# Filler products ahead of waiting TensorE steps: 78 more in the first fifth of an RWKV-7 and SwiGLU kernel

## The chip, the cores and the metric

One core of one Trainium2 chip. The metric is the device time of one execution in microseconds (us), as the median of several runs.

## The reference

Two blocks in a row, all in float32.

```python
# r, k, v, w, a, b: (4 batches, 8 heads, 768 steps, 40)
for t in range(S):
    y[:, :, t] = einsum('bhd,bhde->bhe', rt, state)
    Sa = einsum('bhde,bhe->bhd', state, at)
    state = state * wt[:, :, None, :] - einsum('bhd,bhe->bhde', Sa, bt)
    state = state + einsum('bhd,bhe->bhde', vt, kt)
x = y as (3072 tokens, 320)
xn = x / sqrt(mean(x * x) + 1e-6) * rms_g
out = (silu(xn @ w_gate) * (xn @ w_val)) @ w_out      # 320 -> 1536 -> 320
```

The three weight matrices of the FFN come as float64 and are made float32 on the chip.

## The kernel before, in words

The recurrence is cut into 24 chunks of 32 steps. For a chunk `c` the program makes four groups of steps:

- `front(c)`: loads of `w`, `a` into `wan`, of `k`, `b` into `kbn`, of `v` into `VU` (four loads for `wan`, four for `kbn`, eight for `VU`; from chunk 2 on they stand in POOL's queue), transposes of them by TensorE (`turn`), and for each of the five levels 1, 2, 4, 8, 16 a Gram product (`gram`, 32 matmul records in the trace) whose operand `KE` is copied by ScalarE and whose result is masked into `LT` by VectorE and copied into `KN` by ScalarE. The products by the decays (`K`, `A`, `T`) are VectorE's.
- `early_inverse(c)` for chunks 0 to 3, `inverse(c)` for the others: a triangular inverse, row by row on VectorE (`tmp`, then `Yi` or `M`), after `LT` has gone to DRAM (`sB`) and come back (`M`) through SP's queue; in the early form two TensorE steps (`inv`) put two half inverses together.
- `main(c)`: products with the state (`state`), with `LT` (`lower`), the update of the state (`update`), the scores of `r` (`score`), the output level by level (`y0`, `level`; VectorE adds them up in `y`), and then the transposes `turn4` and `turn3` around the normalisation (ScalarE squares, POOL takes the power, `ss`), which end in the FFN's input `xg`.
- After every second chunk `feed(g)`: the FFN for 256 tokens over twelve slices of the weights: `h64` and `h` (gate and value), `sg` by ScalarE, `hT` by VectorE, and `out`, which accumulates in the PSUM tile `po`.

In the first two chunks there are also 24 `narrow` steps: the weights are loaded as pairs of 32-bit words and made float32 by ScalarE (`ex`) and VectorE (`w`).

The steps are not issued in this order. The functions only note them down as pieces of a plan; `Plan.issue` then goes through the list `ORDER`, written out ahead of time, and issues one piece after the other. Each number counts from the first piece that has not been issued. Each engine works through its own pieces in the order of issue, so that list is the order of every engine and of every queue (SP, ACT and POOL issue the loads). Semaphores are put in by the framework where a piece reads or overwrites what another has made.

A piece that needs PSUM has a "room" of one or two banks; `PAIRS` has one digit for each of the 523 rooms, and says in which of the three bank pairs (0, 2, 4) it lies. The first piece of a room waits until the last reader of the room before it in that bank pair is done.

The sign `-` in `ORDER` is a filler: it calls `plan.warm`, a product of the identity with itself into columns 320 to 447 of `po`, which nothing reads.

```python
            if word == "-":
                self.order.append(None)
                self.warm()
                continue
```

```python
plan.warm = lambda: nc.tensor.matmul(po_[:, 0, DM:DM + P], ident, ident, start=False, stop=False, skip_group_check=True)
```

A float32 product appears in the trace as two records, so a filler is two LDWEIGHTS and two MATMUL of 128x128 by 128x128. The kernel before has 28 fillers: seven ahead of the first FFN step, the rest spread up to the end.

Helpers are recorded under one line each, so the trace's lines read: L499 products, L502 transposes, L1014 fillers (all TensorE); L457 VectorE; L477, L480, L483 ScalarE (activation, copy, scale); L486, L489, L492 POOL; L496 loads and stores.

Of the kernel before, what the change touches and what calls it, by code (L numbers as in the profile page):

```python
# [36 lines left out]
199 96 112 105 61 66 111 115 119 106 116 130 120 117 118 129 - 200 107 121 212 222 211 232 242 131 204 205 208 209 210  # L37
193 472 477 221 35 134 476 132 62 206 213 489 219 207 490 470 471 321 0 216 217 122 43 125 64 124 222 213 - 191 219 214
# [4 lines left out]
501 510 506 503 493 508 517 514 507 519 515 21 22 321 - 520 516 322 263 518 193 817 502 511 521 - 512 525 529 398 1003  # L43
# [5 lines left out]
32 37 406 405 408 293 349 317 - 832 318 1 956 834 418 419 839 344 404 833 598 845 843 409 841 410 350 421 558 559 424  # L49
# [6 lines left out]
428 429 432 589 590 419 408 594 593 592 986 859 591 595 543 596 597 422 598 599 409 600 922 980 - 982 925 854 855 862  # L56
# [9 lines left out]
277 385 222 80 278 769 122 303 279 0 385 279 120 12 122 11 373 575 82 83 222 223 224 232 13 14 307 359 280 386 71 - 281  # L66
387 16 388 389 231 17 0 554 765 430 375 376 60 65 555 556 0 209 764 763 563 264 558 265 562 374 0 374 375 564 376 558
287 100 207 210 211 284 559 377 563 572 265 560 565 571 427 65 1 2 3 0 - 62 570 565 262 1001 425 263 569 562 578 374
375 579 0 0 0 560 202 692 199 207 60 561 208 61 563 577 0 0 371 0 371 372 373 374 375 227 228 376 377 571 565 378 570
59 206 207 420 422 421 569 575 423 379 61 62 380 381 382 383 384 579 385 424 - - 425 - 427 276 271 1 0 0 0 0 381 382 58  # L70
579 0 560 - 0 573 0 380 420 560 577 573 418 381 575 - 568 680 - 578 382 383 559 581 569 582 384 580 595 250 570 385 584
574 386 579 528 527 - 423 431 594 425 424 589 588 387 388 389 390 391 392 393 434 394 395 427 1 2 3 0 0 428 424 421 2
677 680 0 0 44 - 0 387 419 421 423 47 587 426 0 426 427 431 673 674 587 241 714 718 736 242 576 577 428 719 982 715 254
# [3 lines left out]
694 - 943 944 945 360 392 393 394 565 745 395 0 608 691 611 609 610 612 357 709 694 562 697 563 698 692 695 925 461 693  # L77
# [969 lines left out]
```

## Time and profile before

| | |
|---|---|
| median of 3 runs | 933.53 us (932.12 to 934.17) |
| profiled execution | 934.43 us, span from first to last instruction 932.6 us |
| TensorE (PE) busy | 875.3 us, 94% of the span, 22072 matmuls |
| weight loads (PEld) | 700.9 us, 75% |
| VectorE (DVE) busy | 728.2 us, 78% |
| ScalarE (ACT) busy | 522.2 us, 56% |
| GpSimd (POOL) busy | 297.6 us, 32% |
| mean granted TensorE clock | 0.970 |

Read the shares by stages: until about 116 us the recurrence's first chunks and the weights' narrowing share all engines, later the FFN fills TensorE. The busy time of a matmul is from its start to its modelled end, and matmuls overlap; so a burst is read by its start, its length and its count. The clock column says which share of TensorE's full clock was granted, where the trace has a record of it.

### The profile page before, as it was taken

The numbers are of one execution on the slowest core, as the hardware profiler recorded it, in microseconds if no ns is written. First come the engines' busy times: TensorE is split into PE (matmuls) and PEld (weight loads), VectorE is DVE, ScalarE is ACT, GpSimd is POOL, SyncE is SP. The second block draws the span as 40 slices with busy tenths as digits, with TensorE's granted clock in tenths as the row PEclk, the third lists the DMA queues.
The fourth block names the chain that finished last, engine by engine and source line by source line (L and its number), as shares of the span: only waits on it lengthen the run. The fifth ranks groups of instructions, "written<-read, shape, count | busy, mean of one in ns | idle before, by whom it ended". The sixth has DMA issues, their size and how long they took to land.

```text
span 932.6 us, 50209 instructions
## 1 busy us (share of the span) xinstructions
PE 875.3 (94%) x22072; PEld 700.9 (75%) x22072; DVE 728.2 (78%) x2702; ACT 522.2 (56%) x1144; POOL 297.6 (32%) x515
## 2 busy tenths in 40 slices
PE   4766799899999999999999999999999999999998
PEld 4665677678777778778887877778777778777786
DVE  6887889778878988889888887888888878774411
ACT  6887877764574564666556456547455454432211
POOL 7676555413232333233324212514403230020000
PEclk9995599989999999999999999999999999999999
DMA  8654556342233233234323303414404222021000
GB/s 155 111 104 106 126 117 123 79 81 64 48 76 66 52 69 67 53 70 91 68 47 70 77 18 77 94 24 84 93 13 92 59 44 58 7 59 29 2 15 15
DMA packets 146362, 63.00 MB, mean 68 GB/s; under 512 B 128800, under 2 KB 138080, under 8 KB 146144
## 3 DMA queue, kind: packets, MB, share of 16 engines
q1 hardware_dynamic: 125664, 29.46, 16.7%
q0 software_dynamic: 18368, 30.01, 14.7%
q8 instruction: 173, 2.83, 1.3%
q10 hardware_dynamic: 2112, 0.33, 0.3%
q14 instruction: 45, 0.37, 0.1%
HBM read 49.15 MB, written 10.09 MB: 64 GB/s over the span
## 4 chain that ended last, share of the span: by engine, by line
PE 63%; DVE 11%; ACT 9%; issue 7%; DMA 5%; POOL 3%; SPq 1%; DVEq 0%; ACTq 0%; POOLq 0%
PE ps L499 44%; PE po L499 12%; PE ps L502 6%; DVE tmp L457 2%; DMA w<-in_moe_w_out_dram 2%; DVE Yi L457 2%; ACT VU L480 1%; DVE y L457 1%; DVE hT L457 1%; ACT KE L480 1%; SPq L496 1%; DVE w L457 1%; DVE K L457 1%; ACT ex L477 1%; POOL w L496 1%
## 5 line engine op out<-in xcount | busy, mean ns | idle before, releaser
L499 PE MATMUL ps<-xg,w 128*128 128x256 f32 (+1 forms) x1728 | 355.1, 394 | 2.4 <-DVE tmp L457 1.0
L499 PEld LDWEIGHTS ps<-xg,w 128*128 128x128 f32 (+1 forms) x1728 | 265.3, 192 | 51.6 <-issue 12.0
L499 PE MATMUL po<-w,hT 128*128 128x320 f32 x576 | 178.4, 445 | 0.0
L496 POOL DMA_DIRECT2D VU<-in_v_dram x184 | 102.4, 561 | 136.9 <-PE ps L499 97.7
L457 DVE TENSOR_TENSOR tmp<-Yi,M 128x60 f32<-128x60 f32 (+24 forms) x620 | 129.3, 209 | 15.5 <-DMA M<-sB 2.7
L457 DVE TENSOR_TENSOR Yi<-Yi,tmp 128x60 f32<-128x60 f32 (+24 forms) x620 | 129.8, 210 | 14.1 <-DMA rn<-in_r_dram 0.3
L480 ACT COPY KE<-K 128x512 f32<-128x512 f32 x168 | 110.6, 661 | 44.2 <-DVE K L457 36.7
L477 ACT ACTIVATE sg<-ps 128x256 f32<-128x256 f32 x144 | 52.8, 385 | 142.2 <-PE ps L499 133.1
L499 PEld LDWEIGHTS po<-w,hT 128*128 128x128 f32 x576 | 103.6, 189 | 36.7 <-issue 1.3
L457 DVE TENSOR_TENSOR hT<-ps,sg 128x256 f32<-128x256 f32 x144 | 58.6, 420 | 74.5 <-ACT sg L477 72.7
L457 DVE TENSOR_TENSOR K<-K,T 128x256 f32<-128x256 f32 x240 | 98.3, 420 | 13.2 <-ACT KE L480 10.7
L499 PE MATMUL ps<-A,KE 40*64 40x72 f32 x3840 | 94.5, 246 | 13.5 <-ACT A L480 3.9
L499 PEld LDWEIGHTS ps<-A,KE 40*64 40x64 f32 x3840 | 78.5, 148 | 34.1 <-ACT A L480 8.5
L480 ACT COPY KN<-ps 128x320 f32<-128x320 f32 x144 | 67.1, 470 | 63.6 <-DVE LT L457 26.7
L457 DVE COPY_PREDICATED LT<-msk,ps 128x256 f32<-128x256 uint32 x120 | 65.9, 549 | 21.0 <-PE ps L499 16.1
L486 POOL TENSOR_TENSOR ss<-ss,mhalf 128x1 f32<-128x1 f32 x24 | 17.9, 745 | 187.5 <-DVE ss L457 186.3
L457 DVE TENSOR_TENSOR y<-y,ps 128x256 f32<-128x256 f32 x119 | 49.8, 419 | 15.5 <-PE ps L499 12.9
L457 DVE TENSOR_TENSOR A<-A,T 128x128 f32<-128x128 f32 (+1 forms) x168 | 56.0, 337 | 2.7 <-ACT A L480 1.7
L496 POOL DMA_DIRECT2D kbn<-in_k_dram x44 | 29.1, 663 | 85.8 <-PE ps L502 79.7
L499 PEld LDWEIGHTS ps<-As,KN 64*40 64x40 f32 x3840 | 45.8, 123 | 14.1 <-issue 5.1
L499 PE MATMUL ps<-As,KN 64*40 64x32 f32 x3840 | 51.9, 205 | 3.9 <-ACT y L480 1.8
L480 ACT COPY VU<-ps 32x320 f32<-32x320 f32 x96 | 40.0, 417 | 13.9 <-PE ps L499 12.7
(121 smaller groups left out, 1245.0 us busy)
## 6 DMA issues: line engine op xcount, KB each, us to landing
M<-sB SPq DMA_DIRECT2D x80, 128.0 KB, 3.3
rn<-in_r_dram SPq DMA_DIRECT2D x24, 160.0 KB, 3.6
out_dram<-o SPq DMA_DIRECT2D x48, 80.0 KB, 2.9
VU<-in_v_dram POOLq DMA_DIRECT2D x184, 20.0 KB, 2.7
kbn<-in_b_dram POOLq DMA_DIRECT2D x44, 80.0 KB, 3.6
kbn<-in_k_dram POOLq DMA_DIRECT2D x44, 80.0 KB, 3.6
wan<-in_w_dram POOLq DMA_DIRECT2D x44, 80.0 KB, 3.1
wan<-in_a_dram POOLq DMA_DIRECT2D x44, 80.0 KB, 3.1
```

Source lines behind the costliest of these rows:

```text
L457: plan.add("DVE", kind, lambda at: fn(at(o), *m(at)), [o], aps(*args))
L477: plan.add("ACT", "act", lambda at: nc.scalar.activation(at(o), at(a), f, **kw), [o] + aps(acc), [a])
L480: plan.add("ACT", "copy", lambda at: nc.scalar.copy(at(o), at(a)), [o], [a])
L486: plan.add("POOL", "tt", lambda at: nc.gpsimd.tensor_tensor(o, a, b, op), [o], [a, b])
L496: plan.add(by, "dma", lambda at: queue.dma_start(out=o, in_=i), [o], [i])
L499: return o, lhsT, rhs, lambda at: nc.tensor.matmul(at(o), lhsT, rhs, start=start, stop=stop, skip_group_check=True)
L502: return o, i, ident, lambda at: nc.tensor.transpose(at(o), i, ident)
```

## The change

`ORDER` gets 78 more `-`, at 25 places; with the `-` taken out, the list of numbers is the same in both. `PAIRS` differs in 94 of its 523 digits. All code is the same. The places, by the TensorE step that the new fillers stand in front of, in order of issue:

| in front of | new fillers |
|---|---|
| `front(0)` transpose of `KE`; `front(1)` Gram level 1, level 4, level 8; `front(3)` first transpose | 7; 3, 3, 4; 3 |
| `main(0)` first `lower`; `front(2)` Gram level 1, level 4; `early_inverse(0)` first, second `inv`; `front(2)` Gram level 16 | 7; 1, 2; 3, 2; 1 |
| `main(0)` transpose of `VU`, `score`, first `level` | 5, 4, 2 |
| `front(3)` second transpose, Gram level 1 | 1, 6 |
| `main(1)` transpose of `VU`, `score`, first `level`, `turn4`, `turn3` | 2, 1, 3, 8, 3 |
| `main(3)` second `lower`, `update` | 3, 2 |
| `front(5)` Gram level 8; `main(3)` `level` for level 1 | 1; 1 |

The diff, cut to its core (the numbers are the same throughout; the lines are broken anew):

```diff
-199 96 112 105 61 66 111 115 119 106 116 130 120 117 118 129 - 200 107 121 212 222 211 232 242 131 204 205 208 209 210
-193 472 477 221 35 134 476 132 62 206 213 489 219 207 490 470 471 321 0 216 217 122 43 125 64 124 222 213 - 191 219 214
...
+199 96 112 105 61 66 111 115 119 106 116 130 120 117 118 129 - 200 107 121 212 222 211 232 242 - - - - - - - 131 204 -
+- - 205 208 209 210 193 472 477 221 35 134 476 132 62 206 213 489 219 207 490 470 471 321 0 216 217 122 43 125 64 124
+222 213 - 191 219 214 123 - - - 223 229 226 227 230 215 232 490 228 238 236 237 66 242 224 126 127 134 239 135 240 - -
+- - 233 247 243 234 373 374 136 137 138 139 140 141 142 818 474 822 381 225 819 823 35 473 244 - - - 835 143 246 144
...
```

```diff
 PAIRS = """
-20404244230204042223024024202204224244423024242422242000000400040454220222424244000044242440444042200044020420420224240
+20404244230204042223024024202204224244423024242422242000000400040454220222424244000044242440444042200044020240420224240
...
```

Taken room by room in the order of issue, 12 rooms get another predecessor in their bank pair, in six pairs of rooms that swap: two in `front(5)`, one in `main(3)` and one in `main(4)`, then `main(18)` with `feed(7)`, `front(21)` with `main(19)` twice, and `main(21)` with `main(22)`.

More of the change, by code (lines that the diff above doesn't have):

```diff
@@ L36 @@
 92 103 94 90 85 201 370 34 98 77 19 99 100 87 262 133 473 86 102 202 113 104 186 187 101 108 109 203 95 97 110 114 198
-199 96 112 105 61 66 111 115 119 106 116 130 120 117 118 129 - 200 107 121 212 222 211 232 242 131 204 205 208 209 210
-193 472 477 221 35 134 476 132 62 206 213 489 219 207 490 470 471 321 0 216 217 122 43 125 64 124 222 213 - 191 219 214
[4 rows of a table removed]
-501 510 506 503 493 508 517 514 507 519 515 21 22 321 - 520 516 322 263 518 193 817 502 511 521 - 512 525 529 398 1003
[5 rows of a table removed]
-32 37 406 405 408 293 349 317 - 832 318 1 956 834 418 419 839 344 404 833 598 845 843 409 841 410 350 421 558 559 424
+199 96 112 105 61 66 111 115 119 106 116 130 120 117 118 129 - 200 107 121 212 222 211 232 242 - - - - - - - 131 204 -
+- - 205 208 209 210 193 472 477 221 35 134 476 132 62 206 213 489 219 207 490 470 471 321 0 216 217 122 43 125 64 124
+222 213 - 191 219 214 123 - - - 223 229 226 227 230 215 232 490 228 238 236 237 66 242 224 126 127 134 239 135 240 - -
+- - 233 247 243 234 373 374 136 137 138 139 140 141 142 818 474 822 381 225 819 823 35 473 244 - - - 835 143 246 144
+145 146 147 148 149 150 235 258 319 62 1006 195 245 257 151 152 153 251 154 155 156 157 158 397 1002 485 259 836 837
+248 260 63 491 486 30 388 254 67 253 - - - - - - - 310 159 160 161 162 163 252 164 165 166 487 311 376 499 196 190 262
+496 495 249 167 500 498 509 504 505 121 - 492 497 255 256 494 501 510 506 503 493 508 517 514 507 519 515 21 22 321 -
+520 516 322 263 518 193 817 502 - - 511 521 - 512 525 529 398 1003 168 513 522 524 170 174 173 172 176 530 382 19 46
+389 25 - - - 177 377 535 527 178 375 169 523 526 383 189 534 378 528 264 265 266 267 268 269 270 271 31 272 820 29 23
+273 171 175 - - 179 180 391 274 275 538 194 24 50 - 531 545 399 392 312 314 315 316 313 - - - - - 325 546 326 - - - -
+329 532 384 323 324 49 821 385 402 386 533 330 331 - - 336 276 277 278 279 537 280 281 282 283 1007 339 415 400 541 284
+285 407 20 1343 338 286 287 288 289 394 290 416 547 548 401 393 291 335 332 292 47 337 540 539 542 544 333 334 403 340
+395 536 838 396 341 343 543 549 550 551 552 553 554 345 555 556 557 342 346 347 417 420 348 250 48 816 32 37 406 405
+408 293 349 317 - - 832 318 1 956 834 418 419 - - - - - - 839 344 404 833 598 845 843 409 841 410 350 421 558 559 424
 483 957 294 295 560 840 351 296 844 411 425 426 51 423 484 427 428 422 842 846 847 352 297 599 303 300 2 601 433 478
@@ L52 @@
 270 376 819 825 393 827 271 1231 813 377 828 829 526 822 272 824 320 985 837 527 378 528 529 838 530 531 826 831 396
[3 rows of a table removed]
-428 429 432 589 590 419 408 594 593 592 986 859 591 595 543 596 597 422 598 599 409 600 922 980 - 982 925 854 855 862
[9 rows of a table removed]
-277 385 222 80 278 769 122 303 279 0 385 279 120 12 122 11 373 575 82 83 222 223 224 232 13 14 307 359 280 386 71 - 281
-387 16 388 389 231 17 0 554 765 430 375 376 60 65 555 556 0 209 764 763 563 264 558 265 562 374 0 374 375 564 376 558
-287 100 207 210 211 284 559 377 563 572 265 560 565 571 427 65 1 2 3 0 - 62 570 565 262 1001 425 263 569 562 578 374
@@ L69 @@
[L69 to L73, printed above, removed]
[3 rows of a table removed]
@@ L77 @@
-694 - 943 944 945 360 392 393 394 565 745 395 0 608 691 611 609 610 612 357 709 694 562 697 563 698 692 695 925 461 693
[27 rows of a table removed]
-1002 455 1008 1006 946 860 861 859 810 862 811 1015 1016 1162 812 450 - 451 1156 863 813 864 814 815 865 866 867 868
[14 rows of a table removed]
-844 841 436 - 437 843 845 799 442 800 438 982 1095 848 992 983 801 995 993 682 846 851 1003 1001 1002 802 852 984 669
-1008 1012 838 996 430 1139 945 944 685 1142 853 1138 803 1154 - 1000 1009 839 1155 994 1156 854 855 856 1010 1140 1135
[3 rows of a table removed]
-1024 450 1168 445 1171 - 438 1085 942 1025 1175 1181 446 1026 1027 938 1182 1095 669 1180 1028 1194 818 817 816 819
[36 rows of a table removed]
@@ L162 @@
-1051 1192 1217 1178 1052 1093 - 449 1179 669 1187 1053 1054 1188 1055 1189 1395 1056 943 1057 999 1104 1108 1058 1109
-1191 450 451 1059 1060 1106 670 1105 1107 1196 439 443 1203 1061 1193 671 1112 1111 1062 869 870 1110 1144 944 1399
-1197 1114 1063 1064 1198 1113 448 1199 1065 1115 1116 1117 1412 1066 1067 1068 1205 1069 453 1409 1604 1121 1201 941
-942 938 1070 1071 1200 939 1601 1208 1207 1413 1414 1206 1118 1120 1119 - 458 454 1072 1073 1074 1122 1411 1213 1214
-1123 1124 1125 1126 1410 0 452 1420 1073 456 1287 457 453 1072 1207 1206 1208 1209 1212 1199 1412 1213 1285 - 868 1416
[6 rows of a table removed]
@@ L173 @@
-1154 1155 1156 799 800 1398 999 1006 1005 850 851 801 852 802 425 803 804 805 856 857 858 859 - 430 860 861 806 837
[9 rows of a table removed]
-1599 942 941 1067 1202 1209 1208 1211 458 1410 1409 1214 1414 1068 1069 1070 1071 1072 1201 453 447 - 451 454 1215 1073
[53 rows of a table removed]
-280 268 273 277 281 282 285 286 297 292 288 293 289 301 298 302 294 290 291 295 303 299 300 304 0 233 - 0 129 226 227 1
-0 0 225 222 0 0
+273 417 532 823 566 832 567 570 568 569 399 984 400 836 833 - - 573 533 835 426 424 425 443 841 839 534 535 536 537 538
+539 842 843 402 847 834 540 574 401 844 852 853 420 541 542 403 968 964 860 840 846 845 404 321 324 418 423 861 965 -
@@ new lines @@
+577 579 583 580 585 588 581 323 322 407 406 856 427 587 857 421 578 405 850 851 969 - - - 586 444 441 1228 611 858 584
+582 430 431 428 429 432 589 590 419 408 594 593 592 986 859 591 595 543 596 597 422 598 599 409 600 922 980 - 982 925
+854 855 862 924 412 544 413 - - - - - - - - 601 923 981 410 994 602 411 987 571 637 612 603 564 638 640 414 572 546 629
+630 604 991 639 848 605 606 - - - 607 608 609 909 910 613 992 545 610 863 990 993 864 616 865 1004 866 867 868 869 614
[8 rows of a table added]
+13 14 307 359 280 386 71 - 281 387 16 388 389 231 17 0 554 765 430 375 376 60 65 555 556 0 209 764 763 563 264 558 265
@@ new lines @@
+562 374 0 374 375 564 376 558 287 100 207 210 211 284 559 377 563 572 265 560 565 571 427 65 1 2 3 0 - 62 570 565 262
+1001 425 263 569 562 578 374 375 579 0 0 0 560 202 692 199 207 60 561 208 61 563 577 0 0 371 0 371 372 373 374 375 227
+228 376 377 571 565 378 570 59 206 207 - - - 420 422 421 569 575 423 379 61 62 380 381 382 383 384 579 385 424 - - - -
+425 - 427 276 271 1 0 0 0 0 381 382 58 579 0 560 - 0 573 0 380 420 560 577 573 418 381 575 - - 568 680 - 578 382 383
+559 581 569 582 384 580 595 250 570 385 584 574 386 579 528 527 - 423 431 594 425 424 589 588 387 388 389 390 391 392
@@ new lines @@
+393 434 394 395 427 1 2 3 0 0 428 424 421 2 677 680 0 0 44 - 0 387 419 421 423 47 587 426 0 426 427 431 673 674 587 241
+714 718 736 242 576 577 428 719 982 715 254 978 730 432 387 388 257 389 243 429 433 434 244 573 732 - 430 737 435 731
+436 1139 437 438 740 439 582 583 515 1 0 533 534 0 0 471 391 932 3 689 540 541 694 542 543 392 693 695 526 690 342 610
+611 343 544 545 546 547 548 549 550 551 552 341 344 692 553 705 554 702 4 5 555 0 392 346 0 611 554 555 556 557 558 559
+560 561 562 563 564 346 343 263 924 925 344 694 - 943 944 945 360 392 393 394 565 745 395 0 608 691 611 609 610 612 357
[27 rows of a table added]
@@ new lines @@
+809 689 858 1161 1013 1160 454 1002 455 1008 1006 946 860 861 859 810 862 811 1015 1016 1162 812 450 - 451 1156 863 813
[14 rows of a table added]
+792 793 794 795 796 850 797 798 842 844 841 436 - 437 843 845 799 442 800 438 982 1095 848 992 983 801 995 993 682 846
+851 1003 1001 1002 802 852 984 669 1008 1012 838 996 430 1139 945 944 685 1142 853 1138 803 1154 - 1000 1009 839 1155
[3 rows of a table added]
+1019 1020 1167 1083 1021 1022 1023 740 1024 450 1168 445 1171 - 438 1085 942 1025 1175 1181 446 1026 1027 938 1182 1095
[36 rows of a table added]
+1177 1186 1184 1190 1194 1195 1051 1192 1217 1178 1052 1093 - 449 1179 669 1187 1053 1054 1188 1055 1189 1395 1056 943
@@ new lines @@
+1057 999 1104 1108 1058 1109 1191 450 451 1059 1060 1106 670 1105 1107 1196 439 443 1203 1061 1193 671 1112 1111 1062
+869 870 1110 1144 944 1399 1197 1114 1063 1064 1198 1113 448 1199 1065 1115 1116 1117 1412 1066 1067 1068 1205 1069 453
+1409 1604 1121 1201 941 942 938 1070 1071 1200 939 1601 1208 1207 1413 1414 1206 1118 1120 1119 - 458 454 1072 1073
+1074 1122 1411 1213 1214 1123 1124 1125 1126 1410 0 452 1420 1073 456 1287 457 453 1072 1207 1206 1208 1209 1212 1199
+1412 1213 1285 - 868 1416 1417 1418 1215 1216 1217 1074 0 626 1106 981 970 420 964 421 972 978 752 979 976 769 977 696
[6 rows of a table added]
@@ L239 @@
+858 859 - 430 860 861 806 837 1150 431 426 807 808 809 1003 1 810 996 1395 1397 1394 811 424 812 813 1151 838 1004 1164
[9 rows of a table added]
+1071 1072 1201 453 447 - 451 454 1215 1073 1074 1418 1217 1419 1218 1415 1219 1422 459 1421 455 1075 1076 1423 1428
[53 rows of a table added]
+290 291 295 303 299 300 304 0 233 - 0 129 226 227 1 0 0 225 222 0 0
 """
 PAIRS = """
-20404244230204042223024024202204224244423024242422242000000400040454220222424244000044242440444042200044020420420224240
+20404244230204042223024024202204224244423024242422242000000400040454220222424244000044242440444042200044020240420224240
@@ L243 @@
 04002000042242424200000400422404424424424442440222222422004244042044222420022024222024402444202024400020000040200442004
-40042404042022224202220204244400402420440242202440442442224422242222402404240244024242220020202000024444402204244024024
-40020002020042442040420224220042002040242244202220244202404442444242242000004022004442240200444002004002200220402444240
-44002200404242004420022042222240242000402240024
+40042404042022224202220204244400402420440242202440442442224422242222402404240244024242220020202000024444402204244024020
@@ L247 @@
+44420002020042442040420224220042002040202222402220244202040002002242202444440404002224420244022004002004400444204222420
+22004444242024002240400420000024020444240024402
 """
```

328 rows, old and new, of the table ORDER are left out of this document.

## The prediction

> **What bounds the kernel now.** I read the page first: its span, its busy shares and the chain that ended last.
>
> ```profile
> span 932.6 us, 50209 instructions
> ...
> PE 875.3 (94%) x22072; PEld 700.9 (75%) x22072; DVE 728.2 (78%) x2702; ACT 522.2 (56%) x1144; POOL 297.6 (32%) x515
> ...
> PE 63%; DVE 11%; ACT 9%; issue 7%; DMA 5%; POOL 3%; SPq 1%; DVEq 0%; ACTq 0%; POOLq 0%
> ```
>
> TensorE sets the end, but 94% is a mean over unlike stages. The view by stretches (columns: stretch, length, busy us of PE, PEld, DVE, ACT and POOL with counts, granted clock, DMA) parts them.
>
> ```profile
> 10.00:116.00 106.00, 77.82 (x2368) 67.36 (x2365) 88.97 (x289) 87.50 (x183) 69.04 (x124) 0.79 0.57 116
> 260.00:800.00 540.00, 531.33 (x13931) 423.38 (x13921) 458.88 (x1789) 304.78 (x673) 156.85 (x259) 1.00 0.31 62
> ```
>
> From 260 us on TensorE has work all the time at full clock (531 of 540), so whatever is won or lost earlier is carried to the end unchanged. Before 116 us it idles 28.2 of 106 us, VectorE and ScalarE are busier than it is, and the clock is said to be 0.79. That clock flatters: the trace has no clock record before 67.8 us, and the page counts that as full. The durations tell the truth (timeline rows: start, us, instructions).
>
> ```profile
> 29.68 1.24 PE L499 MATMUL ps<-A,KE 40*64 40x72 f32 x32
> ```
> ```profile
> 176.77 0.73 PE L499 MATMUL ps<-A,KE 40*64 40x72 f32 x32
> ```
> ```profile
> 163.63 1.99 PE L499 MATMUL ps<-xg,w 128*128 128x256 f32 x8
> ```
> ```profile
> 170.84 3.35 PE L499 MATMUL ps<-xg,w 128*128 128x256 f32 x8
> ```
>
> A Gram step takes 0.73 us at full clock and 1.24 at 29.68 us; a pair of FFN products 1.99 at full and 3.35 in the stretch marked 0.50. So half clock costs a burst 41% of its half-clock time, and nearly everything before 116 us runs at half clock. What releases it? The next rows have stretches of 3.41 us, cut at the spacing at which the clock changes in the trace, and what products ran in three of them (20.02:23.43, 98.52:101.94, 112.18:115.59, in that order).
>
> ```profile
> 16.60:20.02 3.42, 3.42 (x74) 3.00 (x77) 3.27 (x11) 3.12 (x8) 2.21 (x4) 1.00 0.86 114
> 98.52:101.94 3.42, 3.42 (x160) 3.28 (x162) 2.92 (x7) 3.39 (x7) 0.30 (x1) 0.50 0.55 120
> 112.18:115.59 3.41, 3.06 (x72) 2.21 (x72) 2.56 (x12) 3.41 (x8) 2.04 (x4) 0.50 0.68 117
> 115.59:119.00 3.41, 3.41 (x38) 2.45 (x40) 3.30 (x8) 2.68 (x7) 2.91 (x5) 1.00 0.24 40
> 166.79:170.20 3.41, 1.60 (x116) 1.46 (x119) 3.06 (x13) 2.77 (x8) 1.30 (x2) 1.00 0.22 52
> 170.20:173.62 3.42, 3.42 (x56) 2.79 (x44) 2.91 (x12) 1.87 (x4) 0.00 (x0) 0.50 0.28 97
> ```
>
> ```profile
> L499 PE MATMUL ps<-A,KE 40*64 40x72 f32 x64 | 2.2, 327 | 0.0
> L1014 PE MATMUL po<-ident 128*128 128x128 f32 x2 | 0.8, 500 | 0.0
> ```
> ```profile
> L499 PE MATMUL ps<-As,KN 64*40 64x32 f32 x144 | 2.8, 252 | 1.8 <-ACT y L480 1.8
> ```
> ```profile
> L499 PE MATMUL ps<-xg,w 64*128 64x256 f32 x8 | 2.0, 661 | 0.4 <-ACT xg L483 0.4
> L499 PE MATMUL ps<-VU,LT 32*32 32x40 f32 x64 | 1.3, 263 | 0.0
> ```
>
> Busy time does not decide: 98.52 to 101.94 is busy throughout and the clock stays at half, while 112.18 to 115.59 is less busy and is followed by full clock. What differs is how much of the array is used. Counting rows x columns x streamed columns, without transposes: 144x64x40x32 = 11.8 million, not granted; 64x40x64x72 + 2x128x128x128 = 16.0 million, not granted; 8x64x128x256 + 64x32x32x40 = 19.4 million, granted. One filler is two records of 128x128x128, 4.2 million: four fillers in 3.4 us reach 16.8 million alone, and two beside a few Gram steps do.
>
> **The change part by part.** It removes and moves nothing; it adds 78 products (156 records), 71 of them at 21 places before 116 us and 7 at four places between 168 and 191 us. A filler reads the constant identity and waits for nothing but its turn; it delays what stands behind it on TensorE. Behind TensorE stand others, the software DMA queue among them: a load into kbn is issued by POOL only after the transposes of its old contents (a row of the waits from 10 to 116 us: total, times, longest).
>
> ```profile
> POOL kbn L496 <- PE ps L502: 12.5, 3, 4.3
> ```
>
> The price of a filler: 256 streamed columns cost 1.99/8 = 0.25 us at full clock and 3.35/8 = 0.42 at half; the upper bound is an isolated one, 0.79 (the filler pair at 21.84).
>
> ```profile
> 21.84 0.79 PE L1014 MATMUL po<-ident 128*128 128x128 f32 x2
> 23.80 1.07 PE L502 MATMUL ps<-ident,KE 40*128 40x40 f32 x16 [1.16 <-ACT KE L480]
> 25.44 1.24 PE L499 MATMUL ps<-A,KE 40*64 40x72 f32 x32 [0.57 <-ACT KE L480]
> 26.61 1.10 PE L502 MATMUL ps<-ident,kbn 64*104 64x64 f32 x16
> 27.63 1.24 PE L499 MATMUL ps<-A,KE 40*64 40x72 f32 x32
> ```
> ```profile
> 24.55 0.84 ACT L480 COPY KE<-K 128x512 f32<-128x512 f32 x1
> ```
>
> (1) 21 to 29 us. Seven fillers stand before the transpose at 23.80, which idled 1.16: 2.9 us at half clock (+1.8), 1.75 at full (+0.6). They are what brings the grant, at one of the clock's 3.4-us edges, so I take the middle, +1.2. ScalarE's copy at 24.55 overwrites KE, which that transpose reads, and ScalarE works in order without a pause behind it, so nothing covers the delay. Three more before the Gram step at 25.44 (idle 0.57) cost 0.2 to 0.7, say 0.4. Against it, the unbroken burst from 25.44 to 28.87 is 41% of 3.43 = 1.4 shorter if the grant is there: half of it, -0.6. Sum +1.0; ends -0.6 (0.6+0.2-1.4) and +6.2 (isolated price: 4.4+1.8).
>
> ```profile
> 35.24 1.18 PE ps L502 x16
> ...
> 48.06 1.27 PE ps L499 x32
> ...
> 58.02 1.11 PE ps L502 x16
> ```
>
> (2) 28 to 71 us. The chain of waits has only these three TensorE pieces here; the rest is VectorE, ScalarE and DMA. At full clock 41% of 3.56 goes: -1.5. The fillers at 14 places fit their idle time at 0.25 each, so they cost nothing there, and VectorE's in-order work is late next. Ends: -1.5, and 0 if the clock falls back.
>
> ```profile
> 89.44 1.09 PE L502 MATMUL ps<-ident,VU 64*104 64x64 f32 x16 [0.68 <-ACT VU L480]
> ```
>
> (3) 71 to 98 us gets three fillers at two places, too few for full clock: 3x0.42 less the idle 0.68 is +0.6; ends 0 and +1.3 (no cover).
>
> ```profile
> by line: PE ps L499 30.5%; PE ps L502 19.9%; ACT ex L477 6.7%; POOL ss L486 6.1%; ACT rE L480 5.6%; issue 5.2%; ACT r L480 5.1%; ACT xg L483 3.7%; ACT M L483 3.6%; ACT A L480 3.6%; ACT x L483 3.0%; ACT T L480 2.7%; ACT x L477 2.4%; ACT y L4
> ```
>
> ```profile
> 105.91 0.65 PE L502 MATMUL ps<-ident,y 40*128 40x40 f32 x8 [0.88 <-DVE y L457]
> ```
> ```profile
> 108.13 0.44 ACT L477 ACTIVATE x<-ps 128x320 f32<-128x320 f32 x1
> ```
>
> (4) 98 to 116 us (the first row is the chain by line there): TensorE holds 50.4% of 18 us, 9.1 us. At full clock throughout that gives -3.7. If the grant comes only with the eight fillers before 105.91, these take 3.4 us at half clock against 0.88 idle, 2.5 late; 1.6 of it is covered by ScalarE, which reads that transpose (ended 106.56) only at 108.13; what follows gains about 1.3. I take -2.0; ends -3.7 and +2.5.
>
> (5) 168 to 198 us. The half-clock products at 170.84 lose 3.35-1.99 = 1.4. Those from 193.01 to 197.51, where the clock returns, lose 41% of 4.5 = 1.8.
>
> ```profile
> 193.01 6.93 PE L499 MATMUL ps<-xg,w 64*128 64x256 f32 x24
> ```
>
> Three fillers go into the stretch that lost the clock (12.6 million, 1.60 busy of 3.41 before), one into the later one. I take half of 3.2 as saved, less 4x0.25 = 1.0 for four fillers on a now saturated TensorE, of which half is covered: -1.2; ends -3.2 and +1.0.
>
> (6) PSUM banks. Matching steps to the trace in issue order, 12 of 523 tiles get another predecessor. The worst: a transpose at 674.17 would wait for the gate product that ended 675.32, which today holds the FFN step behind it.
>
> ```profile
> 675.38 2.84 PE L499 MATMUL ps<-xg,w 64*128 64x256 f32 x15 [0.55 <-DVE hT L457]
> ```
>
> Since that step already idles 0.55 for the same release, only the transpose's rest is added: +0.3; ends -0.5 and +1.2.
>
> Sum: +1.0 -1.5 +0.6 -2.0 -1.2 +0.3 = -2.8 us. The profiled execution took 934.4 (span 932.6), so 931.6; it stands 0.9 above the median of the runs shown, 933.5, and against that the forecast is 930.7.
>
> **The rivals.** *Fillers without clock, slower.* A filler at half clock is as long as the idle time it is put into, or longer: 71 of them are 29.8 us against 28.2 us of idle time before 116 us. If the grant does not hold between 27 and 67 us, each place overruns. With about half the fillers' time uncovered and half of that on the chain, +7: 941. It decides if more than half of the fillers run at half clock. For it: the stretch of 16.0 million that was not granted. Against it: four fillers make 16.8 without any other work. The Trainium skill, "TensorE: Matmul & The Clock Gate", section "HAM oscillation — how this bites in real kernels", gives as its rule that no idle gap on TensorE over some 3.4 us keeps the clock. By that rule the fillers change no clock, since no gap after 13 us is that long, and the change is pure cost. This trace goes against it: 16.60 to 20.02 is busy to the end, and the Gram step at 29.68 still takes 1.24.
>
> *Clock without gain, the same.* VectorE is busy 89 and ScalarE 87.5 of the 106 us. If their order binds everywhere, terms 2 and 4 shrink to some -1.5 together while 1, 3 and 6 stay: -0.8, 932.7.
>
> *Full clock throughout, much faster.* If the density of work at full clock keeps the grant from 25 us on, term 4 gives -3.7, term 5 -3.2, term 1 0 and 71 to 98 us about -1: -9, 924.5.
>
> **How the numbers follow.** About 0.2% (1.9 us) is what can be told from no change. The forecast (a gain of 2 to 6 us) has 0.42, full clock throughout 0.11, clock without gain 0.25, fillers without clock 0.10, and late grants whose overruns outweigh the gains (terms 1, 3 and 4 near their upper ends, 936 to 938) 0.12. So faster 0.53, same 0.25, slower 0.22. The likeliest alone is 927.5 to 931.5. The range, 925 to 938, leaves out the upper rival and most of the lowest.
>
> **What would show it.** Right: the Gram steps of the second and third chunk take 0.73 instead of 1.24; clock records show a grant before 30 us; the stage up to the first FFN product (113.72) ends 2 to 4 us earlier; the products at 170.84 take 1.99. Wrong: fillers spaced 0.2 us per record after 30 us; the first FFN product no earlier, with idle time before it moved from TensorE's waits to the fillers; a wait on VectorE or ScalarE that is longer by what TensorE saved; a new idle gap near 674 us over 1 us.

## The result: slower by 3.7%, and the profile after

The changed kernel took 968.65 us in the median of 3 runs (966.55 to 984.86), against 933.53 before: 1.0368 times as long, 95% interval 1.0329 to 1.0406. The forecast was 930.7, the range 925 to 938; the measured time lies 31 us above it. Lines of the file have moved by one, so the products are now L500, the transposes L503, the fillers L1015. The profiled execution is the longest of the three, 984.86 us, and was a disturbed one: its delays are read for their shape, and the size of the effect is taken from the experiments.

The page after, with the row of the code-loading queue, which the prediction did not look at (packets, MB, share of the DMA engines):

```profile
span 983.0 us, 50521 instructions
...
PE 908.8 (92%) x22228; PEld 723.9 (74%) x22228; DVE 728.2 (74%) x2702; ACT 521.6 (53%) x1144; POOL 295.4 (30%) x515
...
q8 instruction: 174, 2.85, 1.2%
...
PE 68%; issue 9%; DVE 8%; ACT 7%; DMA 4%; POOL 2%; SPq 1%; ACTq 0%; DVEq 0%; POOLq 0%
```

And the same queue before:

```profile
q8 instruction: 173, 2.83, 1.3%
```

TensorE's busy time went up by 33.5 us, of which the records of the fillers are 26.8 (41.2 us against 14.4), and its idle time by 16.9 (74.2 us against 57.3); in the chain that ended last "issue" rose from 7% to 9%, which is time in which an engine waited for nothing that the profile names. The view by stretches says where (the same two stretches as in the prediction):

```profile
10.00:116.00 106.00, 85.51 (x2408) 74.94 (x2405) 84.68 (x275) 83.32 (x173) 65.23 (x118) 0.81 0.55 112
260.00:800.00 540.00, 514.62 (x13328) 406.21 (x13329) 436.97 (x1703) 289.20 (x641) 150.81 (x251) 0.98 0.30 60
```

Most of the loss is not where the fillers are. Between 260 and 800 us, where no filler was added, TensorE now idles 25.4 of 540 us (8.7 before), its clock is 0.98 instead of 1.00, and it gets through 13328 products instead of 13931. Early on the fillers did what they were to do to the clock (timeline rows: start, us, instructions; before, the Gram step took 1.24 and the FFN products 3.35):

```profile
27.71 0.73 PE L500 MATMUL ps<-A,KE 40*64 40x72 f32 x32
...
29.17 0.73 PE L500 MATMUL ps<-A,KE 40*64 40x72 f32 x32
...
170.41 1.99 PE L500 MATMUL ps<-xg,w 128*128 128x256 f32 x8
```

Matching each TensorE step of the old order to itself in the new trace gives its delay:

```text
start before, us   32   71   100  136  167  190  210  225  249  313  337  end
delay after, us   1.7  5.2  4.9  7.0  6.4  7.9  9.4 13.5 14.6 18.1 22.3 50.4
```

It is a staircase that climbs to the end: flat for tens of microseconds, then a step. At each step stands a stall like this one (timeline; in brackets the idle time ahead and its releaser), and the stretches around it (columns as in the prediction):

```profile
231.05 0.34 PE L500 MATMUL ps<-As,KN 64*40 64x32 f32 x11 [2.16 <-issue]
```
```profile
229.00:231.05 2.05, 0.00 (x0) 0.00 (x0) 1.76 (x8) 1.98 (x4) 0.00 (x0) 1.00 0.30 50
231.30:234.70 3.40, 3.40 (x15) 2.75 (x9) 2.43 (x8) 0.00 (x0) 0.00 (x0) 0.51 0.27 63
234.70:238.10 3.40, 3.40 (x15) 2.77 (x15) 0.89 (x4) 1.06 (x3) 0.00 (x0) 0.99 0.47 130
```

TensorE stops dead for 2.16 us in the middle of a burst of equal products that wait for nobody, and then runs 3.4 us at half clock (0.51). The view of waits sums these stalls up, before and after (us in total, times, longest):

```profile
PE ps L499 <- issue: 2.7, 3, 1.1
```
```profile
PE ps L500 <- issue: 24.1, 24, 2.5
...
PE ps L503 <- issue: 5.8, 4, 1.9
...
PE po L500 <- issue: 1.7, 3, 1.2
```

3 stalls of 2.7 us in all have become 31 of 31.6 (29 of them last over 0.25 us). What they have in common is found by counting TensorE's instructions up to each, in the trace:

```text
after, resumed at us    71.03 189.40 200.98 231.05 323.19 353.28 482.93 675.48
idle ahead, us           2.46   1.56   1.27   2.16   1.14   1.80   1.88   1.73
TensorE instruction no.  2496   8385   8896  10433  14784  16320  22977  32705
no. modulo 256            192    193    192    193    192    192    193    193
last load begun, us ago  2.67   2.55   2.41   2.62   2.19   2.35   2.45   2.33
```

All 29 stalls over 0.25 us, of which these are eight, and the three before too, stand at an instruction whose number is 192 or 193 modulo 256, and end 2.2 to 3.1 us after the start of the last transfer of the queue "instruction". Its 173 packets before carry 2.83 MB, 16384 bytes each; TensorE's program has 44384 instructions before (22072 weight loads, as many matmuls, 240 others), and 44384/256 = 173.4. After it is 44696, 174.6 blocks, 174 packets. So the queue brings TensorE's program, 256 instructions at a time. In the traces of before and after the closest two of its loads start 3.30 and 3.24 us apart. A block that TensorE runs through faster than that leaves it without instructions: 24 of the 29 stalls stand behind a block that was spent in 1.5 to 3.1 us. The other five blocks lasted 3.5 to 6.9 us.

The spacing does not look like a limit of the queue itself. When the load that TensorE waited for began, the load ahead of it was 3.7 to 11.8 us old in these 29 cases. But it began only after TensorE had entered the block it was running, a median 1.0 us behind that block's first instruction, and TensorE went on at least 2.2 us after that; the two make up the 3.2 us. So the traces fit a lead of one block. For the five longer blocks the load began 1.6 to 5.0 us behind the block's start, and for the three stalls of before 1.8 to 3.0 us; why so late was not found.

Eight FFN products take 1.99 us, so a block of 128 such takes 32; but a block of the small products can be spent in under 2 us, as in this row of before:

```profile
217.53 0.79 PE L499 MATMUL ps<-As,KN 64*40 64x32 f32 x63
```

Before, the shortest time between two block edges is 3.2 us; after, the shortest that ends in a stall is 1.5 us. A filler is four instructions, so 78 of them are 312 = 256 + 56: every block edge after 198 us lies 56 instructions earlier in the work than before, and dense bursts that were parted by an edge now fall into one block.

The Trainium skill, "Runtime: NRT & Kernel Launch", section "Instruction fetch mechanics", says that the program comes in blocks of 256 instructions of 16 KiB, and that crossing an edge is mostly hidden. The first is what the 16384-byte packets show; the second holds before (3 stalls of 173 edges) and fails after, where the measurement decides: 31 stalls, 31.6 us.

### The profile page after: what moved, and what is told of

It is laid out like the page before. It is cut to its first block, busy times and chain, and to the rows that moved or that the text cites. A ratio compares the mean times of both kernels' runs of the same rounds, so it can differ in the third digit from the quotient of the medians.

```text
span 983.0 us, 50521 instructions
## 1 busy us (share of the span) xinstructions
PE 908.8 (92%) x22228; PEld 723.9 (74%) x22228; DVE 728.2 (74%) x2702; ACT 521.6 (53%) x1144; POOL 295.4 (30%) x515
## 4 chain that ended last, share of the span: by engine, by line
PE 68%; issue 9%; DVE 8%; ACT 7%; DMA 4%; POOL 2%; SPq 1%; ACTq 0%; DVEq 0%; POOLq 0%
PE ps L500 46%; PE po L500 14%; PE ps L503 7%; DVE tmp L458 1%; PE po L1015 1%; DMA w<-in_moe_w_out_dram 1%; ACT VU L481 1%; DVE hT L458 1%; DVE Yi L458 1%; SPq L497 1%; DVE w L458 1%; DVE LT L458 1%; ACT sg L478 1%; ACT ex L478 1%; DVE y L458 1%
## 5 line engine op out<-in xcount | busy, mean ns | idle before, releaser
L500 PE MATMUL ps<-xg,w 128*128 128x256 f32 (+1 forms) x1728 | 362.0, 398 | 4.8 <-issue 2.2
L500 PEld LDWEIGHTS ps<-xg,w 128*128 128x128 f32 (+1 forms) x1728 | 269.2, 194 | 57.5 <-issue 16.0
L500 PE MATMUL po<-w,hT 128*128 128x320 f32 x576 | 186.9, 461 | 1.7 <-issue 1.7
L458 DVE TENSOR_TENSOR tmp<-Yi,M 128x60 f32<-128x60 f32 (+24 forms) x620 | 128.9, 208 | 16.7 <-DMA M<-sB 4.1
L458 DVE TENSOR_TENSOR Yi<-Yi,tmp 128x60 f32<-128x60 f32 (+24 forms) x620 | 129.5, 209 | 14.4 <-DVE Yi L458 0.3
L500 PEld LDWEIGHTS po<-w,hT 128*128 128x128 f32 x576 | 106.9, 196 | 41.4 <-issue 7.7
L500 PE MATMUL ps<-A,KE 40*64 40x72 f32 x3840 | 90.9, 237 | 17.6 <-issue 5.5
L500 PEld LDWEIGHTS ps<-A,KE 40*64 40x64 f32 x3840 | 74.8, 140 | 38.4 <-issue 13.8
L500 PEld LDWEIGHTS ps<-As,KN 64*40 64x40 f32 x3840 | 46.3, 123 | 17.4 <-issue 11.7
L500 PE MATMUL ps<-As,KN 64*40 64x32 f32 x3840 | 52.8, 205 | 6.2 <-issue 5.6
L481 ACT COPY VU<-ps 32x320 f32<-32x320 f32 x96 | 39.9, 416 | 17.9 <-PE ps L500 16.8
```

The costliest lines, as they stand in the source:

```text
L458: plan.add("DVE", kind, lambda at: fn(at(o), *m(at)), [o], aps(*args))
L481: plan.add("ACT", "copy", lambda at: nc.scalar.copy(at(o), at(a)), [o], [a])
L500: return o, lhsT, rhs, lambda at: nc.tensor.matmul(at(o), lhsT, rhs, start=start, stop=stop, skip_group_check=True)
```

## The experiments

The theory: the loss is the phase of the block edges, that is, where in the work they fall, with what the stalls do to the clock. The rivals: the fillers themselves (their time, or dense work early that makes the clock fall later), and the new PSUM banks. Several kernels use a "tiny" product, four instructions like a filler but one column wide on 32 rows, in all but one of them put at one place, between the steps that start at 190.9 and 191.4 us in the kernel before; it shifts the edges behind it and does next to no work:

```diff
+            if word == ".":
+                self.order.append(None)
+                self.tiny()
+                continue
...
+    plan.tiny = lambda: nc.tensor.matmul(po_[0:32, 0, DM:DM + 1], ident[0:32, 0:32], ident[0:32, 0:1], start=False, stop=False, skip_group_check=True)
```

**14 tiny products in the kernel before (56 instructions).** The order and banks are the old ones.

```diff
-978 730 432 387 388 257 389 243 429 433 434 244 573 732 430 737 435 731 436 1139 437 438 740 439 582 583 515 1 0 533
+978 730 432 387 388 257 389 243 429 433 434 244 573 732 430 . . . . . . . . . . . . . . 737 435 731 436 1139 437 438
```

> The kernel before with 14 one-column products (56 TensorE instructions, no other change) at one place near 190 us, where TensorE idles 0.8 us. Theory of code loading: the instructions come in blocks of 256, the block edges after that place fall where they fall in the changed kernel, and from the trace of before 27 to 29 blocks there would be used up in under 3.2 to 3.5 us, the shortest spacing of block loads; 27 to 36 us longer in all, so 960 to 970, with TensorE stalls at instruction numbers 192 modulo 256. Rival, the fillers' own work and clock: 14 tiny products cost under 1 us, so 933 to 935.

Measured: 975.95 us, 1.0454 times the kernel before (1.0407 to 1.0501); more than the 960 to 970 expected, which had counted the stalls and not the clock. Its waits for nothing, and the inserted products:

```profile
PE ps L503 <- issue: 19.2, 19, 2.3
...
PE ps L506 <- issue: 6.2, 5, 2.3
...
PE po L503 <- issue: 1.2, 2, 0.8
```
```profile
191.51 1.04 PE L1019 MATMUL po<-ident 32*32 32x1 f32 x28
```

Fourteen products that last 1.0 us together cost 42. No added filler and no new bank is needed for the loss. The delay is 0.2 us at 202 us and climbs in steps to 41.7. 25.6 us of that are stalls behind the place; the clock records show half clock for 23.9 us behind them (six times, each beginning at a stall or within 2 us behind it), which at the 41% that a burst loses at half clock is 9.8. Together 35 of 42; the rest is idle time that the stalls knock on to, and was not taken apart.

**The kernel after with its 78 new fillers made tiny.** Same number of instructions as after, almost none of the array work.

```diff
-... 232 242 - - - - - - - 131 204 -
-- - 205 208 ...
+... 232 242 . . . . . . . 131 204 .
+. . 205 208 ...
```

> The changed kernel with each of its 78 new fillers made a one-column product: the same number of instructions at the same places, next to no work. Code loading: the late stalls stay, 27 us and more, and the early loss shrinks by the fillers' own time: 958 to 968. Rival, the fillers' work: nearly all of the loss goes, 933 to 937.

Measured: 979.39 us, 1.0469 (1.0404 to 1.0533); above the 958 to 968 expected, and 11 us above after itself, for which no cause was sought. The profiled execution, 970.03 us, is the shortest of the four:

```profile
PE ps L504 <- issue: 20.3, 18, 2.0
...
PE ps L507 <- issue: 4.8, 5, 1.9
...
PE po L504 <- issue: 1.3, 3, 0.6
```

At least as slow as after, so the loss is not the time of the fillers nor what they do to the clock.

**50 tiny products more in the kernel after (312 + 200 = 512 instructions).** All of the change is kept, and the edges are put back.

```diff
-... 732 - 430 737 435 ...
+... 732 - 430 . . . (50 of them) . . . 737 435 ...
```

> The changed kernel with 50 one-column products (200 instructions) at the same place near 197 us, so that 312 + 200 = 512 instructions stand ahead of all that follows and the block edges fall as in the kernel before. Code loading: the loss up to there (about 8 us) stays, the stalls after it go: 940 to 945. Rival, the fillers' work and a clock upset by it: 968 to 972.

Measured: 944.98 us, 1.0105 (1.0066 to 1.0144).

```profile
PE ps L505 <- issue: 8.5, 8, 1.7
```
```profile
196.40 4.33 PE L1021 MATMUL po<-ident 32*32 32x1 f32 x100
```

Adding work to the slow kernel takes some 24 us off it. Of its stalls only 1.4 us lie behind the inserted products, where after has 25 us; the delay there is flat, 8.5 us at 210 and 10.5 at the end. Ahead of them the delay is already 5.1 us: 5.0 + 2.1 us of stalls stand there among the fillers, where the edges still lie wrong (1.7 us in the kernel before). The tiny products add 4.1.

**7, 28 and 64 tiny products in the kernel before (28, 112 and 256 instructions).** The same edit with another count. What each count should do can be counted on the trace of before: move every edge behind that place by so many instructions, and add up what each block's time falls short of 3.2 us. That gives 0 for 0 and for 252, 16.9 us for 28, 27.7 for 56, and the most, 55.1, for 112. Of the 64 shifts by whole products only four (248, 252, 0 and 4) come to under 1 us, and all from 28 to 228 to over 15: the old order lies in a narrow valley, and an edit that ignores the edges is likely to leave it.

> The kernel before with 7 one-column products (28 instructions) at the place near 190 us. Code loading: counted on the trace of before, 17 blocks would be used up faster than a load's shortest spacing of 3.2 to 3.5 us, by 17 to 22 us in all; with the clock that the stalls cost, as in the version with 14 (26 us of stalls, 42 slower), 950 to 965. Rival: no order in the shift, any change of the stream costs about the same, 975.

> The kernel before with 28 one-column products (112 instructions) at the same place. Code loading: 40 blocks too fast, 54 to 66 us of stalls, the worst shift there is; 995 to 1020. Rival, any shift costs about the same: 975.

> The kernel before with 64 one-column products (256 instructions, a whole block) at the place near 190 us. Code loading: the edges after it fall as in the kernel before, so only the products themselves are paid, and one more block load: 935 to 940, although this adds over four times as many instructions as the version with 14. Rival (every added instruction costs): four times what the 14 cost.

The waits for nothing behind 200 us with 112, then all of them with 28 and with 256:

```profile
PE ps L503 <- issue: 39.7, 27, 2.3
...
PE ps L506 <- issue: 9.7, 8, 1.9
...
PE po L1018 <- issue: 1.5, 1, 1.5
PE po L503 <- issue: 1.4, 1, 1.4
```
```profile
PE ps L503 <- issue: 10.6, 11, 1.8
...
PE ps L506 <- issue: 2.2, 3, 1.0
...
PE po L503 <- issue: 1.6, 2, 0.9
```
```profile
PE ps L504 <- issue: 2.2, 3, 1.1
```
```profile
193.13 6.68 PE L1020 MATMUL po<-ident 32*32 32x1 f32 x128
```

```text
tiny products   instructions   us (median)   ratio (95%)                 stalls behind the place: counted / measured
 7               28             951.17       1.0184 (1.0155 to 1.0213)   16.9 / 12.5
14               56             975.95       1.0454 (1.0407 to 1.0501)   27.7 / 25.6
28              112            1026.47       1.0986 (1.0954 to 1.1017)   55.1 / 52.5
64              256             943.09       1.0092 (1.0062 to 1.0121)    0   /  1.5
```

The 7 came out within what was expected, the 28 and the 64 some 6 and 3 us above it. This parts the theory from every rival that goes by the amount of work: 28 tiny products cost 92 us, 64 of the same cost 9. In the profiled execution of the 64 the delay behind them is 9.2 us: 1.7 stood there ahead of them, the products (the row at 193.13) add 6.6, and a half clock that lasts longer adds 0.9. From there the delay stays between 9.1 and 10.1 to the end. With 28 products the loss exceeds the stalls by most: 61 us of half clock behind 204 us, a cost of some 25 at 41%, which with 52.5 of stalls and 2.1 for the products themselves is 80 of 92. The clock column of its stretch shows that too, and so few products done in it (13931 before):

```profile
260.00:800.00 540.00, 498.87 (x12458) 390.21 (x12454) 410.60 (x1601) 274.13 (x606) 139.93 (x232) 0.95 0.28 57
```

**The new banks alone.** The old order with the new `PAIRS`.

```diff
 PAIRS = """
-...424244000044242440444042200044020420420224240
+...424244000044242440444042200044020240420224240
...
```

> The kernel before with the changed kernel's PSUM banks and nothing else: 12 PSUM tiles get another predecessor. All theories: 933 to 936, at most one new wait of about 1 us near 674 us. If the banks had a part in the loss of 35 us, 940 or more.

Measured: 935.23 us, 1.0011 (0.9996 to 1.0026). The place that the prediction named, by the timeline:

```profile
676.92 0.66 PE L502 MATMUL ps<-ident,rn 64*104 64x64 f32 x16 [0.99 <-ACT KN L480]
```

The transpose waits, as foreseen, 0.99 us; over the steps around it (663 to 694 us) the delay grows by 0.47.

**64 of the 78 fillers (256 instructions).** Fourteen are left out of the kernel after at nine places: two of the five ahead of `inv` in `early_inverse(0)`, the one at `front(2)` level 16, one and two at the transposes of `VU`, two of three at `main(1)` `level`, three of eight at `turn4`, one of two at `update`, and the last two places whole.

```diff
-... 381 575 - - 568 680 - 578 ...
+... 381 575 - 568 680 - 578 ...
...
-413 - - - - - - - - 601 923
+413 - - - - - 601 923
...
```

> The changed kernel with 64 instead of 78 new fillers (14 taken away at nine places from 52 us on, where the edges of the blocks then meet the least dense stretches), so that exactly 256 instructions are added and all later block edges stand as in the kernel before. Code loading plus a clock that the fillers lift: the late stalls go without any padding, 929 to 936. If the fillers' own time were the loss: 64/78 of 35 us, 962.

Measured: 935.35 us, 1.0010 (0.9989 to 1.0031): the same as before, and 33 us faster than with 78. It is the version that could have beaten both, and it does not beat the old one. Its waits for nothing, and its two stretches:

```profile
PE ps L500 <- issue: 3.3, 5, 1.3
...
PE ps L503 <- issue: 0.7, 1, 0.7
```
```profile
10.00:116.00 106.00, 83.26 (x2471) 73.17 (x2468) 86.27 (x282) 84.62 (x178) 68.02 (x122) 0.78 0.55 113
...
260.00:800.00 540.00, 530.44 (x13983) 423.06 (x13984) 457.67 (x1787) 304.59 (x673) 155.04 (x259) 1.00 0.31 63
```

The late stretch is that of before again (530 of 540, clock 1.00), so this kernel shows what the fillers are worth without the shift of the late edges. Delays of its steps against before:

```text
start before, us   24   32   65   71   78   101  106  112  119  158  176  202  210  end
delay, us         1.7  1.2  1.3  3.8  2.2  2.6  2.9  2.4  4.2  4.1  0.6  1.9  1.9  2.5
```

How much of such a delay is chance can be seen on the versions with 7, 14, 28 and 64 tiny products and on that with the new banks: up to 190 us their TensorE program is that of before, in the same order. Their delays against the same trace of before, lowest and highest of the five:

```text
start before, us   32          71          98          114         119         158         176
delay, us          0.2 to 1.3  0.1 to 1.9  0.1 to 1.8  0.1 to 1.3  1.6 to 2.1  1.4 to 2.2  0.0 to 1.7
```

So one trace does not tell a delay of under some 2 us from chance, and the trace of before is the quickest of the six at nearly all of these points.

## Why the prediction was wrong, step by step

The step that failed is the first sentence of the change part by part: "It removes and moves nothing", with a filler's price as what it "delays" behind it. 312 added instructions move every block edge behind them. With that fell the sentence on the stage after 260 us, that "whatever is won or lost earlier is carried to the end unchanged": the change cost 41 of the 50 us of its profiled delay behind 210 us, where it had added nothing. No rival had it either. The profile before had both halves of it in sight: a queue called "instruction" with 173 packets of 16 KB, and three waits "issue" in the middle of bursts.

The terms, by the one trace of the kernel with 64 fillers, since after mixes them with late stalls; no size of under 2 us is sure, as shown above:

- **(1) 21 to 29 us, +1.0.** The mechanism was right: full clock from 26 us on, and this Gram step at 0.73. In the version with the new fillers made tiny, the step at the same place still takes 1.24 (second row), so it is the fillers' work that brought the clock. The delay at 32 us, +1.2, agrees with the term, but the unchanged program shows 0.2 to 1.3 there in the five traces above:

```profile
28.63 0.73 PE L500 MATMUL ps<-A,KE 40*64 40x72 f32 x32
```
```profile
27.80 1.24 PE L504 MATMUL ps<-A,KE 40*64 40x72 f32 x32
```

- **(2) 28 to 71 us, -1.5.** Wrong, and above its upper end, 0: the delay goes from 1.2 to 1.3 at 65 us and to 3.8 at 71, of which 0.7 is a stall at an edge. The clock was won at 26.0, then fell at 49.9 for 10 us, and with the fall the fillers stopped being free, against the term's "they cost nothing there". In the chain of waits of this kernel a Gram step and four fillers at half clock stand on the path, ahead of 51 products:

```profile
50.15 1.24 PE ps L500 x32
51.38 2.00 PE po L1015 x8
53.39 0.69 PE ps L500 x51
```

- **(3) 71 to 98 us, +0.6.** Not as forecast: the peak at 71 us is taken back by idle time behind it, so the delay falls to 2.2 at 78 us and stands at 2.6 at 101, -1.2 in all; (2) and (3) together are +1.4 where -0.9 was forecast. At 71 us after has its first large stall, 2.46 us.
- **(4) 98 to 116 us, -2.0.** Wrong. The grant came with the eight (here five) fillers, at 107.9, as one branch of the term had it, within this burst, but was withdrawn from 114.7 to 121.6, where the trace of the old kernel had full clock: the delay is 2.4 us before it and 4.2 behind. Between 98 and 122 us it was at half for 16.7 us, and 17.6 before: the clock was moved, not gained. Some 1 us of the growth is no work of the fillers, since the five versions with the same program lose 0.8 to 1.5 there too.

```profile
106.83 2.11 PE L1015 MATMUL po<-ident 128*128 128x128 f32 x12
```

- **(5) 168 to 198 us, -1.2.** The mechanism was right: the products that took 3.35 take 1.99. The delay falls by 2.2 from 158 to 202 us, but with the new banks alone it falls by 3.3, so the size is not shown:

```profile
172.70 1.99 PE L500 MATMUL ps<-xg,w 128*128 128x256 f32 x8
```

  In after, stalls of 1.56 and 1.27 us at 189 and 201 us ate it.
- **(6) Banks, +0.3.** Right in place and size: +0.47 there; what all the banks cost, 1.0011 times the time before (0.9996 to 1.0026), is not told from nothing.

Sum of (1) to (5): forecast -3.1, measured +1.9 at 210 us, of which 1.3 are early stalls beyond those of before (2.0 against 0.7 ahead of the first FFN step). The medians agree: 1.0010 times the kernel before, between -1.0 and +2.9 us by the interval, where the forecast for all 78 was -2.8. So for the fillers alone the number of the rival "clock without gain" held (-0.8 forecast); whether its reason did, that the order of VectorE and ScalarE binds, is not shown. VectorE's busy time in the stretch hardly moved (89.0 to 86.3), and the first FFN step starts 2.5 us later, at 116.24. What binds it there was not tried.

Three sums of the prediction are slightly off, without weight: half of 1.4 is 0.7 and not 0.6 in (1), (5) comes to -1.1 and not -1.2, and the -0.8 of "clock without gain" needs term (5) beside those it names. Its four fillers at 16.8 million were also never measured to be enough: its own rows leave open what lies between 16.0 and 19.4.

Of the signs named: the early grant and the 1.99 came true, and in after eight of the ten Gram steps of the second and third chunk at 0.73; the last two, at 50.01 and 56.35 us, took 0.89 and 1.24. Of the signs of being wrong, "fillers spaced 0.2 us per record after 30 us" came true from 50 to 60 us (58.92 us: ten records in 2.21). The first FFN step came 4.5 us later (118.26), not 2 to 4 earlier. "A new idle gap near 674 us over 1 us" came true by name and not by cause: in after it is 1.73 us "issue", at instruction 32705, an edge.

The rule that the prediction weighed, of the Trainium skill, "TensorE: Matmul & The Clock Gate", section "HAM oscillation — how this bites in real kernels", that no idle gap over some 3.4 us keeps the clock, has the traces against it again: in after eight stalls of 1.0 to 2.2 us behind 200 us were followed or cut by half clock, which before did not have between 197.5 and 931 us.

## What to carry to other kernels

Adding or removing a few TensorE instructions moves the block edges in all that follows, and where TensorE is near saturation nothing hides the stalls: count them, and keep the total shift at a multiple of 256, or count on the trace which blocks become shorter in time than the closest code loads, 3.2 us here. Look for waits "issue" in the middle of bursts, take their instruction numbers modulo 256, and read the delay of matched steps along the whole span: a staircase far behind the edit does not come from the work that was added. A cheap control, a handful of near-empty products at one place, parts "what was added" from "where it pushed the rest".

## What the runs showed of the hardware that was not expected

- TensorE's code comes in blocks of 256 instructions. In after, the load that a stall waited for began a median 1.0 us after TensorE had entered the block before it, and TensorE went on 2.2 to 3.0 us later; no two loads began less than 3.24 us apart. A block spent sooner stalls it, here for up to 2.5 us at an edge. 28 near-empty products cost 92 us by that and by the clock.
- A stall of 1 to 2.5 us can cost the clock as well: half clock for 3.4 or 6.8 us behind it (0.51 after the stall at 231 us). With 112 instructions added, 61 us of half clock came that way.
- Unbroken work does not bring the clock back by itself: 128 one-column records ran without a pause (193.13 to 199.81 us, with 64 tiny products), and the half clock that began at 193.9 us lasted until 207.6; in the kernel before, with FFN products there instead, it lasted from 190.7 to 197.5.
